# Attention loop of a graph transformer on one core: another order of VectorE's small steps and of the value weighting

## The chip, the cores and the metric

One core of a Trainium2 chip (trn2) runs one program. Its engines are TensorE (PE: matrix products, with a weight load PEld ahead of each), VectorE (DVE), ScalarE (ACT), GpSimd (POOL) and SyncE (SP, which issues DMAs). Each engine takes its own instructions strictly in order and waits for others by semaphores. PE writes to PSUM; a PSUM tile must be read out before its buffer can be written again. The metric is the device time of one execution in microseconds, lower is better.

## What is computed

10,000 nodes, 160,000 edges, 128 features. Seven rounds of normalised propagation over the edges give each node 8 tokens; then one attention block over these 8 tokens, and a readout.

```python
h = x; toks = [x]
for _ in range(7):
    msg = h[src] * deg_inv_sqrt[src, None] * deg_inv_sqrt[dst, None]
    h = segment_sum(msg, dst, N); toks.append(h)
tok = stack(toks, axis=1)                      # (N, 8, D)
t = layernorm(tok)
q, key, v = t @ wq, t @ wk, t @ wv             # per token
attn = softmax(einsum('nkd,nld->nkl', q, key) / sqrt(D))
o = tok + einsum('nkl,nld->nkd', attn, v) @ wo
r = layernorm(o)
alpha = softmax(einsum('nkd,d->nk', r, w_r))
out = einsum('nk,nkd->nd', alpha, o)
```

## The kernel before

The seven propagations (class `Hops`) take the first five sixths of the span and are not touched. The attention stage (function `attention`) works on 625 blocks of 128 rows; a row is one token, so a block is 16 nodes of 8 tokens. Blocks go in groups of `SG` = 16 (the first group has one block): 40 groups, `sgs`.

The order of all engines' work in this stage is the order in which the program states it (`manual_schedule`); tile pools add only the semaphore waits. The loop at the end of `attention` is a software pipeline, `for i in range(-1, n + 5)`. Round `i` handles several groups at once, each at another stage:

- group `i + 3`: `load`, eight DMAs from SP
- group `i + 1`: `xT`, PE transposes `pt`, four blocks in each of four quarters, copied by ACT
- group `i`: `val` (PE `pv`, three blocks at a time, copied by ACT), `uT` (PE `pu`, copied by ACT), `score` (PE `ps`, many small 32x32 products); `squares` on ACT gathers the sums of squares, some of group `i` and some of `i + 1`
- group `i - 1`: the softmax, by small VectorE steps. `soft1a` masks the scores and folds them by two additions, `soft1b` scales by `rk`, takes the maximum and subtracts it, `soft_exp` is ACT's exponential, `soft2` sums, inverts and scales, and has GpSimd spread the result to `p4`; `soft2b` gives the row sums `w`; `soft3` transposes on VectorE and has GpSimd copy four pieces into `PT`
- group `i - 2`: `attend` (PE `po`, value weighting, four blocks in each quarter) and `resid` (VectorE, adds the token; it frees the PSUM buffer of `po`, of which there are two)
- group `i - 3`: `stats`, one `bn_stats` of VectorE for each block; `norms`, `root` (ACT) and `norms2` make the inverse deviations of this group's output and of group `i`'s input
- group `i - 4`: `read1`, `read_exp`, `read2`, the softmax of the readout
- group `i - 5`: `read3` (PE `pf`) and `store`

`same_node` (PE `sm`) sums over the rows of a node: in one PSUM tile first the part that the softmax of group `i - 1` reads (`rb`), then the part that the readout of group `i - 4` reads (`lb`). Its inputs `rb` and `lb` are the last results of `norms2` in the round before.

The four quarters `q` of a round stand on PE in this order, `A0` to `A3` being the four calls of `attend`:

| quarter | PE |
|---|---|
| 0 | pt, pv, sm, pv, pf, pv, A0 |
| 1 | pt, pv, pv, pv, A1 |
| 2 | pt, pu, pu, A2 |
| 3 | pt, pu, pu, A3, ps |

On VectorE the order is: `soft1a`, `soft1b`, eight `bn_stats`, `resid` 0, `soft2`, `soft2b`, `read1`, eight `bn_stats`, `resid` 1, `soft3`, `norms`, `read2`, `norms2`, `resid` 2 and 3.

Of the kernel before, what the change touches and what calls it, by code (L numbers as in the profile page):

```python
# [7 lines left out]
F32 = mybir.dt.float32  # L8
# [5 lines left out]
ALU = mybir.AluOpType  # L14
# [894 lines left out]
def attention(ctx, att, out):  # L909
# [33 lines left out]
    def xT(i, q):  # L943
        a, b = 4 * q, min(4 * q + 4, sgs[i][1])
        if q == 0:
            S[i]["xT"] = tp.tile([128, SG, 128], F32, name="xT")
        if a >= b:
            return
        p = pp.tile([128, 4, 128], F32, name="pt", tag="a", bufs=3)
        for g in range(a, b):  # L950
            T.transpose(p[:, g - a, :], S[i]["x"][:, g, :], ident)  # L951
        A.copy(S[i]["xT"][:, a:b, :], p[:, :b - a])  # L952
# [11 lines left out]
    def val(i, c):  # L964
        a, b = 3 * c, min(3 * c + 3, sgs[i][1])
        if c == 0:
            S[i]["v"] = vp.tile([128, SG, 131], F32, name="v")
        if a >= b:
            return
        p = pp.tile([128, 512], F32, name="pv", tag="a", bufs=3)[:, :393].rearrange("p (g d) -> p g d", d=131)  # L970
        for g in range(a, b):
            T.matmul(p[:, g - a, :], S[i]["xT"][:, g, :], Wv, start=True, stop=True)  # L972
        A.copy(S[i]["v"][:, a:b, :], p[:, :b - a])
# [43 lines left out]
        S[i]["rb"] = r  # L1017


    def soft1a(i):  # L1020
        n = sgs[i][1]
        c = wp.tile([128, SG, 4, 8], F32, name="c4")[:, :n]
        V.tensor_tensor(c, S[i]["s"][:, :n].rearrange("p g (n k) -> p g n k", k=8),
                        in4[:, None, :, None].to_broadcast([128, n, 4, 8]), op=ALU.mult)
        d = wp.tile([128, SG, 2, 8], F32, name="c2")[:, :n]
        V.tensor_tensor(d, c[:, :, 0:2], c[:, :, 2:4], op=ALU.add)
        e = S[i]["e"] = wp.tile([128, SG, 8], F32, name="e")[:, :n]
        V.tensor_tensor(e, d[:, :, 0], d[:, :, 1], op=ALU.add)

    def soft1b(i):  # L1030
        n = sgs[i][1]
        e = S[i]["e"]
        rk = wp.tile([128, SG, 8], F32, name="rk")[:, :n]
        V.tensor_tensor(rk, S[i]["sm"][:, 0, :n], S[i]["rs"][:, :, None].to_broadcast([128, n, 8]), op=ALU.mult)
        V.tensor_mul(e, e, rk)
        m = wp.tile([128, SG], F32, name="m")[:, :n]
        V.tensor_reduce(m, e, axis=X, op=ALU.max)
        V.tensor_tensor(e, e, m[:, :, None].to_broadcast([128, n, 8]), op=ALU.subtract)

    def soft_exp(i):  # L1040
        n = sgs[i][1]
# [4 lines left out]
    def soft2(i):  # L1046
        n = sgs[i][1]
        e = S[i]["e"]
        z = wp.tile([128, SG], F32, name="z")[:, :n]
        V.tensor_reduce(z, e, axis=X, op=ALU.add)  # L1050
        V.reciprocal(z, z)
        V.tensor_tensor(e, e, S[i]["sm"][:, 0, :n], op=ALU.mult)
        V.tensor_tensor(e, e, z[:, :, None].to_broadcast([128, n, 8]), op=ALU.mult)  # L1053
        p = wp.tile([128, SG, 4, 8], F32, name="p4")[:, :n]
        G.tensor_tensor(p, e[:, :, None, :].to_broadcast([128, n, 4, 8]), in4[:, None, :, None].to_broadcast([128, n, 4, 8]), op=ALU.mult)  # L1055
        S[i]["p"] = p

    def soft2b(i):

        n = sgs[i][1]  # L1060
        y = S[i]["y"]
        V.tensor_tensor(y[:, :, :8], S[i]["e"], S[i]["sm"][:, 1, :n], op=ALU.mult)
        w = S[i]["w"] = sp.tile([128, SG], F32, name="w")[:, :n]
        V.tensor_reduce(w, y, axis=X, op=ALU.add)

    def soft3(i):
        n = sgs[i][1]
# [12 lines left out]
    def norms(i, j):  # L1080
        v = sp.tile([128, 2, SG], F32, name="rv")
        if not (ok(i) and ok(j)) or min(sgs[i][1], sgs[j][1]) < SG:
            V.memset(v, 1.0)
        if ok(i):
            n = sgs[i][1]
            d = sp.tile([128, SG], F32, name="rx")[:, :n]
            V.tensor_mul(d, S[i]["v"][:, :n, 130], S[i]["v"][:, :n, 130])
            V.scalar_tensor_tensor(v[:, 0, :n], S[i]["sq"][:, :n], 1.0 / D, d, op0=ALU.mult, op1=ALU.subtract)
        if ok(j):
            n = sgs[j][1]  # L1090
            st = S[j]["st"][:, :n]
            d = sp.tile([128, SG], F32, name="rd")[:, :n]
            V.tensor_tensor(d, st[:, :, 1], st[:, :, 4], op=ALU.subtract)
            V.scalar_tensor_tensor(d, d, 0.25, d, op0=ALU.mult, op1=ALU.mult)
            V.tensor_tensor(v[:, 1, :n], st[:, :, 2], st[:, :, 5], op=ALU.add)
            V.scalar_tensor_tensor(v[:, 1, :n], v[:, 1, :n], 1.0 / D, d, op0=ALU.mult, op1=ALU.add)
        V.tensor_scalar(v, v, 1e-5, None, op0=ALU.add)
        return v

# [20 lines left out]
    def read1(i):  # L1120
        n = sgs[i][1]
        lc = S[i]["lc"]
        m = wp.tile([128, SG], F32, name="rm")[:, :n]
        V.tensor_reduce(m, lc, axis=X, op=ALU.max)
        e = S[i]["re"] = wp.tile([128, SG, 9], F32, name="re")[:, :n]
        V.tensor_tensor(e[:, :, :8], lc, m[:, :, None].to_broadcast([128, n, 8]), op=ALU.subtract)
        V.tensor_tensor(e[:, :, 8], S[i]["l"], m, op=ALU.subtract)

    def read_exp(i):
        A.activation(S[i]["re"], S[i]["re"], AF.Exp)  # L1130
# [36 lines left out]
    load(1)  # L1167
    for i in range(-1, n + 5):

        if ok(i + 3):  # L1170
            load(i + 3)
        if ok(i - 1):
            soft1a(i - 1)
        for q in range(4):
            if ok(i + 1):
                xT(i + 1, q)
            if q == 0 and i < 0:
                A.preload_act_table_set("natural_log_exp_and_others")

            cs = range(3 * q, 3 * q + 3) if q < 2 else ()  # L1180
            if ok(i):
                for c in cs[:1]:
                    val(i, c)
            if q == 0:
                if ok(i):
                    squares(i, 9, 11)
                sm = pp.tile([128, 4, SG * 8], F32, name="sm", tag="m", bufs=1).rearrange("p a (g k) -> p a g k", k=8)
                if ok(i - 1):
                    S[i - 1]["sm"] = sm
                    m = sgs[i - 1][1]  # L1190
                    same_node(sm[:, 0:2, :m], S[i - 1]["rb"][:, :, :m])
                if ok(i - 4):
                    m = sgs[i - 4][1]
                    S[i - 4]["lc"] = sm[:, 2, :m]
                    same_node(sm[:, 2, :m], S[i - 4]["lb"][:, :m])
                if ok(i - 1):
                    soft1b(i - 1)
            if ok(i):
                for c in cs[1:2]:
                    val(i, c)  # L1200
            if q == 0:
                if ok(i):
                    squares(i, 11, 12)
                if ok(i - 1):
                    soft_exp(i - 1)
                if ok(i):
                    squares(i, 12, 13)
                if ok(i - 5):
                    read3(i - 5)
            elif q == 1 and ok(i - 5):  # L1210
                store(i - 5)
            if ok(i):
                for c in cs[2:]:
                    val(i, c)
            if q == 0 and ok(i):
                squares(i, 13, 15)
            if q == 1 and ok(i - 4):
                read_exp(i - 4)
            if q == 1 and ok(i):
                squares(i, 15, 16)  # L1220

            for c in range(2 * q - 4, 2 * q - 2) if q >= 2 else ():
                if ok(i):
                    uT(i, c)
                if c == 3:
                    vy.append(root(vy[0]))
                if ok(i + 1):
                    squares(i + 1, *((0, 2), (2, 3), (3, 4), (4, 9))[c])
            if ok(i - 2):
                attend(i - 2, q)  # L1230
            if q == 3 and ok(i):
                score(i)

            if q < 2 and ok(i - 3):
                stats(i - 3, 8 * q, 8 * q + 8)
            if q == 2:
                vy = [norms(i, i - 3)]
                if ok(i - 4):
                    read2(i - 4)
            if q == 3:  # L1240
                norms2(i, i - 3, *vy)
                if ok(i - 2):
                    resid(i - 2, 2)
            if q != 2 and ok(i - 2):
                resid(i - 2, q)
            if q == 0 and ok(i - 1):
                soft2(i - 1)
                soft2b(i - 1)
            if q == 0 and ok(i - 4):
                read1(i - 4)  # L1250
            if q == 1 and ok(i - 1):
                soft3(i - 1)

@with_exitstack
def nagphormer_kernel(ctx, tc, x, src, dst, dis, wq, wk, wv, wo, w_r, out):
# [42 lines left out]
```

## Time and profile before

| | |
|---|---|
| median of 3 runs | 3991.8 us (3988.98 to 3993.97) |
| profiled execution | 3999.62 us, its span 3997.8 us |
| mean granted TensorE clock in it | 0.973 |
| busy: PE, DVE, ACT, POOL | 94%, 83%, 68%, 44% of the span |

The page cuts the span in 40 equal slices; the attention stage is the last seven. Rows of the timeline read: start in us from the span's beginning, duration of the run of equal instructions in us, engine, line of the kernel, operation, output<-inputs, shapes, count; in brackets the idle time of the engine ahead of it and what ended it. A block of f32 products takes two instructions on PE, so `x8` is four blocks. An end on PE is modelled: the next row may start before it. Tiles that lie in the hop tables' memory are named `tab` (the tokens `x` and the outputs `o`).

### The profile page before, as it was taken

Reading aid. Unit: us, or ns where it says so; the run is one execution under the profiler, and the core shown is the slowest. Engines: PE = TensorE matmul, PEld = TensorE weight load, DVE = VectorE, ACT = ScalarE, POOL = GpSimd, SP = SyncE. Lnnn points to the kernel's source line nnn. Section 1 sums busy time; section 2 is a strip of 40 time slices with the busy share of each in tenths; the row PEclk is TensorE's granted clock in tenths of the full one; section 3 lists DMA queues with packets and bytes.
Section 4 is the critical chain, followed back from the end, with each engine's and each line's share of the span. In section 5 each row is a group of like instructions: output and inputs, shape, how many; then the busy total and the mean of one; then the engine's idle time right before and its main releaser. Section 6 shows DMA issues by size and latency. Waiting matters only on the chain.

```text
span 3997.8 us, 165094 instructions
## 1 busy us (share of the span) xinstructions
PE 3745.5 (94%) x69690; PEld 3031.4 (76%) x69690; DVE 3322.9 (83%) x6961; ACT 2724.5 (68%) x6830; POOL 1766.6 (44%) x2342
## 2 busy tenths in 40 slices
PE   6886799999989999999999999999999999999997
PEld 4665566666658888888888788878878887788885
DVE  8998999999977777777777777777766666999998
ACT  6884456666666666666666666666665658888884
POOL 0000333333335665666666566656656662222222
PEclk8998899999999999999999999999999999999998
DMA  3100445454556666666666666666656552222220
GB/s 104 32 2 1 134 151 154 149 162 143 156 168 189 201 201 193 202 203 200 193 202 202 185 202 202 202 189 198 202 184 205 186 183 77 74 74 76 78 78 13
DMA packets 321189, 594.93 MB, mean 149 GB/s; under 512 B 56183, under 2 KB 214101, under 8 KB 315189
## 3 DMA queue, kind: packets, MB, share of 16 engines
q1 hardware_dynamic: 282485, 506.62, 40.0%
q0 software_dynamic: 35392, 72.55, 6.3%
q8 instruction: 546, 8.95, 0.9%
q10 hardware_dynamic: 2560, 5.12, 0.4%
q14 instruction: 206, 1.69, 0.1%
HBM read 455.43 MB, written 128.67 MB: 146 GB/s over the span
## 4 chain that ended last, share of the span: by engine, by line
PE 71%; DVE 19%; ACT 4%; issue 2%; DMA 2%; POOL 0%; another core or an unknown queue 0%; SPq 0%; DVEq 0%; ACTq 0%; POOLq 0%
PE p L580 26%; PE acc L556 24%; PE acc L542 4%; DVE w L514 3%; PE pv L972 3%; PE po L983 3%; PE pu L961 3%; DVE ux L219 2%; DVE o L212 2%; ACT rs L340 2%; PE tb L440 2%; PE pt L951 1%; DVE oh L206 1%; DVE R L212 1%; DVE w L511 1%
## 5 line engine op out<-in xcount | busy, mean ns | idle before, releaser
L585 ACT CAST eb<-p 128x512 f16<-128x512 f32 x3065 | 1623.7, 596 | 645.4 <-PE p L580 404.3
L587 DVE TENSOR_TENSOR eb<-p,one 128x512 f16<-128x512 f32 x1912 | 1230.6, 685 | 332.2 <-PE acc L556 195.9
L580 PE MATMUL p<-tab,w 128*32 128x256 f16 x39816 | 1288.7, 274 | 44.2 <-issue 21.4
L556 PE MATMUL acc<-eb,w 128*128 128x256 f16 (+1 forms) x9954 | 1246.9, 274 | 8.4 <-DVE indeg L649 3.1
L580 PEld LDWEIGHTS <-w 128*32 128x32 fp8e4 x39816 | 1002.3, 96 | 261.3 <-issue 225.8
L556 PEld LDWEIGHTS <-w 128*128 128x128 fp8e4 x9954 | 954.3, 98 | 170.3 <-issue 54.9
L526 POOL DMA_INDIRECT og<-tabh,oidx x553 | 613.3, 1109 | 767.7 <-DVE vi L478 389.6
L526 POOL DMA_INDIRECT og<-tabd,oidx x541 | 586.3, 1084 | 640.2 <-PE acc L556 294.3
L625 POOL TENSOR_SCALAR r<-s,ctok 128x128 f32<-128x128 f32 x474 | 294.3, 621 | 47.7 <-DVE s L571 30.3
L616 ACT ACTIVATE tab<-s,c 128x128 f16<-128x128 f32 x395 | 158.6, 402 | 209.7 <-DVE eb L587 185.6
L617 DVE SCALAR_TENSOR_TENSOR tab<-s,c,tab 128x128 f16<-128x128 f32 x395 | 138.9, 352 | 180.8 <-issue 168.0
L571 DVE TENSOR_REDUCE s<-acc 128x128 f32<-128x256 f32 x553 | 228.7, 414 | 24.0 <-PE acc L569 11.2
L997 ACT ACTIVATE junk<-tab 128x128 f32<-128x128 f32 x625 | 245.1, 394 | 0.0
L340 ACT ACTIVATE rs<-iof,rb 128x128 fp8e4<-128x128 f32 x784 | 231.8, 389 | 0.3
L514 DVE TENSOR_TENSOR w<-dsl,iof 128x2432 fp8e4<-128x2432 f16 x79 | 211.5, 2678 | 0.0
L983 PEld LDWEIGHTS po<-v,pT 128*128 128x128 f32 x1250 | 159.5, 194 | 42.1 <-issue 27.7
L525 POOL COPY og<-eb 128x1 f16<-128x1 f16 x452 | 83.9, 186 | 241.7 <-ACT eb L585 241.7
L1055 POOL TENSOR_TENSOR p<-e,in 128x512 f32<-128x512 f32 (+1 forms) x40 | 40.8, 1020 | 321.0 <-DVE e L1053 321.0
L972 PE MATMUL pv<-Wv,xT 128*128 128x131 f32 x1250 | 176.7, 285 | 1.3 <-ACT xT L952 0.6
L983 PE MATMUL po<-v,pT 128*128 128x128 f32 x1250 | 167.0, 277 | 5.5 <-DVE tab L989 4.1
L972 PEld LDWEIGHTS pv<-Wv,xT 128*128 128x128 f32 x1250 | 154.2, 192 | 17.9 <-issue 8.8
L542 PE MATMUL acc<-og,w 128*128 128x256 f16 x553 | 156.8, 284 | 0.0
(285 smaller groups left out, 4611.9 us busy)
## 6 DMA issues: line engine op xcount, KB each, us to landing
w<-gsd SPq DMA_DIRECT2D x474, 592.0 KB
gsd<-w SPq DMA_DIRECT2D x79, 592.0 KB
rb<-srow SPq DMA_DIRECT2D x79, 576.0 KB
tok<-r SPq DMA_DIRECT2D x546, 64.0 KB
tab<-tok SPq DMA_DIRECT2D x273, 128.0 KB
tabd<-tab SPq DMA_DIRECT2D x396, 64.0 KB
og<-tabh,oidx POOLq DMA_INDIRECT x553
og<-tabd,oidx POOLq DMA_INDIRECT x541
```

Of the source, the lines that this page charges most:

```text
L340: A.activation(ro[:, j - a, i, :], self.iof, AF.Abs_reciprocal_sqrt, scale=2.0 ** 21, bias=rb[:, j - VP, i:i + 1], saturate=False)
L514: V.tensor_tensor(w[:, :NJ * 128].rearrange("p (j d) -> p j d", d=128), dsl[:, g, :, None].to_broadcast([128, NJ, 128]), self.iof1[:, None ...
L526: self.nc.gpsimd.indirect_dma_start(out=o, out_offset=None, in_=src[0] if i == NI else src[1], in_offset=bass.IndirectOffsetOnAxis(ap=self ...
L542: T.matmul(acc[0][:, :256], W, og[i], start=start, stop=stop)
L556: T.matmul(acc[0][:, :m], w[:, J * 128:(J + 1) * 128], e[:, j, :m], start=first and J == 0, stop=J == NG - 1 and not (first or late))
L580: T.matmul(p[32 * q:32 * q + 32, j], w[:, NJ * 128 + s * CAP:NJ * 128 + (s + 1) * CAP], tab[:, s, :], start=True, stop=True)
L585: A.copy(e[:, :n, 0:256], pv)
L587: V.tensor_tensor(e[:, :n, 0:256], pv, self.one[:, :, None].to_broadcast([128, n, 256]), op=ALU.mult)
L625: self.nc.gpsimd.tensor_scalar(r, s, ct[:, t:t + 1], None, op0=ALU.mult)
L972: T.matmul(p[:, g - a, :], S[i]["xT"][:, g, :], Wv, start=True, stop=True)
L983: T.matmul(p[:, g - a, :], PT[i % 2][:, g, :], S[i]["v"][:, g, :128], start=True, stop=True)
L997: A.activation(j, S[i]["x"][:, g, :], AF.Square, bias=S[i]["x"][:, g, 0:1], scale=-1.0, accum_out=S[i]["sq"][:, g:g + 1])
```

## The change

Nothing is computed otherwise. What changes is where steps stand:

- `soft1a` and `soft1b` become one list of steps `soft1`, stated behind `same_node`. `rk`, which reads `sm`, moves from behind both additions to ahead of them.
- `soft1`, `soft2`, `soft2b` and `read1` return their steps as lists. `fill` states them one by one with one `bn_stats` behind most of them: `bn(m)` states the next `m` of the group's sixteen. Ten stand there; one is stated ahead of `soft3`, and the last five behind it, while GpSimd copies its four pieces.
- In `soft2` the product `e` times `sm` moves ahead of the reciprocal. `read1` moves ahead of `soft2`. In `norms` the steps of the two groups alternate.
- `attend` opens each quarter instead of ending it; `score` comes directly behind the last `uT`.
- `resid` 0 comes behind `soft2b`, `resid` 1 behind the last `bn_stats`, `resid` 2 ahead of `norms`, `resid` 3 ahead of `norms2`.

| quarter | PE after |
|---|---|
| 0 | A0, pt, pv, sm, pv, pf, pv |
| 1 | A1, pt, pv, pv, pv |
| 2 | A2, pt, pu, pu |
| 3 | A3, pt, pu, pu, ps |

The core of the diff, with the new loop in place of the old one (the old one is printed above):

```diff
-    def soft1a(i):
...
-    def soft1b(i):
...
+    def soft1(i):
...
+        return (
+            lambda: V.tensor_tensor(c, S[i]["s"][:, :n].rearrange("p g (n k) -> p g n k", k=8),
+                                    in4[:, None, :, None].to_broadcast([128, n, 4, 8]), op=ALU.mult),
+            lambda: V.tensor_tensor(rk, S[i]["sm"][:, 0, :n], S[i]["rs"][:, :, None].to_broadcast([128, n, 8]), op=ALU.mult),
+            lambda: V.tensor_tensor(d, c[:, :, 0:2], c[:, :, 2:4], op=ALU.add),
+            lambda: V.tensor_tensor(e, d[:, :, 0], d[:, :, 1], op=ALU.add),
+            lambda: V.tensor_mul(e, e, rk),
+            lambda: V.tensor_reduce(m, e, axis=X, op=ALU.max),
+            lambda: V.tensor_tensor(e, e, m[:, :, None].to_broadcast([128, n, 8]), op=ALU.subtract))
...
+        return (lambda: V.tensor_reduce(z, e, axis=X, op=ALU.add),
+                lambda: V.tensor_tensor(e, e, S[i]["sm"][:, 0, :n], op=ALU.mult),
+                lambda: V.reciprocal(z, z),
+                last)
...
+        def bn(m):
+            a, b = done[0], min(16, done[0] + m)
+            done[0] = b
+            if ok(i - 3) and a < b:
+                stats(i - 3, a, b)
+
+        def fill(steps, ms):
+
+            for step, m in zip(steps, ms):
+                step()
+                bn(m)
...
+        if ok(i - 2):
+            attend(i - 2, 0)
+        if ok(i + 1):
+            xT(i + 1, 0)
...
+        if soft:
+            fill(soft1(i - 1), (0, 0, 1, 1, 1, 1, 0))
...
+        bn(2)
+        if read:
+            fill(read1(i - 4), (1, 0, 0))
+        if soft:
+            fill(soft2(i - 1), (0, 1, 1, 0))
+            fill(soft2b(i - 1), (1, 0))
+        if ok(i - 2):
+            resid(i - 2, 0)
+
+        if ok(i - 2):
+            attend(i - 2, 1)
...
+        bn(1)
+        if soft:
+            soft3(i - 1)
+        bn(16)
+        if ok(i - 2):
+            resid(i - 2, 1)
...
+        if ok(i - 2):
+            attend(i - 2, 2)
+        if ok(i + 1):
+            xT(i + 1, 2)
+        if ok(i - 2):
+            resid(i - 2, 2)
+        vy = [norms(i, i - 3)]
+        if read:
+            read2(i - 4)
+        u((0, 1))
+
+        if ok(i - 2):
+            attend(i - 2, 3)
+        if ok(i + 1):
+            xT(i + 1, 3)
+        u((2, 3))
+        if ok(i):
+            score(i)
+        if ok(i - 2):
+            resid(i - 2, 3)
+        norms2(i, i - 3, *vy)
```

More of the change, by code (lines that the diff above doesn't have):

```diff
@@ L1049, in soft2, with last @@
         z = wp.tile([128, SG], F32, name="z")[:, :n]
[L1050 to L1056, printed above, removed]
+        p = S[i]["p"] = wp.tile([128, SG, 4, 8], F32, name="p4")[:, :n]
+        def last():
+            V.tensor_tensor(e, e, z[:, :, None].to_broadcast([128, n, 8]), op=ALU.mult)
+            G.tensor_tensor(p, e[:, :, None, :].to_broadcast([128, n, 4, 8]), in4[:, None, :, None].to_broadcast([128, n, 4, 8]), op=ALU.mult)
+        return (lambda: V.tensor_reduce(z, e, axis=X, op=ALU.add),
+                lambda: V.tensor_tensor(e, e, S[i]["sm"][:, 0, :n], op=ALU.mult),
+                lambda: V.reciprocal(z, z),
+                last)
     def soft2b(i):
@@ L1061, in soft2b @@
         y = S[i]["y"]
-        V.tensor_tensor(y[:, :, :8], S[i]["e"], S[i]["sm"][:, 1, :n], op=ALU.mult)
         w = S[i]["w"] = sp.tile([128, SG], F32, name="w")[:, :n]
-        V.tensor_reduce(w, y, axis=X, op=ALU.add)
+        return (lambda: V.tensor_tensor(y[:, :, :8], S[i]["e"], S[i]["sm"][:, 1, :n], op=ALU.mult),
+                lambda: V.tensor_reduce(w, y, axis=X, op=ALU.add))
     def soft3(i):
@@ L1083, in norms @@
             V.memset(v, 1.0)
+        if ok(j):
+            m = sgs[j][1]
+            st = S[j]["st"][:, :m]
+            f = sp.tile([128, SG], F32, name="rd")[:, :m]
+            V.tensor_tensor(f, st[:, :, 1], st[:, :, 4], op=ALU.subtract)
         if ok(i):
@@ L1087, in norms @@
             V.tensor_mul(d, S[i]["v"][:, :n, 130], S[i]["v"][:, :n, 130])
+        if ok(j):
+            V.scalar_tensor_tensor(f, f, 0.25, f, op0=ALU.mult, op1=ALU.mult)
+            V.tensor_tensor(v[:, 1, :m], st[:, :, 2], st[:, :, 5], op=ALU.add)
+        if ok(i):
             V.scalar_tensor_tensor(v[:, 0, :n], S[i]["sq"][:, :n], 1.0 / D, d, op0=ALU.mult, op1=ALU.subtract)
         if ok(j):
[L1090 to L1096, printed above, removed]
+            V.scalar_tensor_tensor(v[:, 1, :m], v[:, 1, :m], 1.0 / D, f, op0=ALU.mult, op1=ALU.add)
         V.tensor_scalar(v, v, 1e-5, None, op0=ALU.add)
@@ L1123, in read1 @@
         m = wp.tile([128, SG], F32, name="rm")[:, :n]
-        V.tensor_reduce(m, lc, axis=X, op=ALU.max)
         e = S[i]["re"] = wp.tile([128, SG, 9], F32, name="re")[:, :n]
-        V.tensor_tensor(e[:, :, :8], lc, m[:, :, None].to_broadcast([128, n, 8]), op=ALU.subtract)
-        V.tensor_tensor(e[:, :, 8], S[i]["l"], m, op=ALU.subtract)
+        return (lambda: V.tensor_reduce(m, lc, axis=X, op=ALU.max),
+                lambda: V.tensor_tensor(e[:, :, :8], lc, m[:, :, None].to_broadcast([128, n, 8]), op=ALU.subtract),
+                lambda: V.tensor_tensor(e[:, :, 8], S[i]["l"], m, op=ALU.subtract))
     def read_exp(i):
@@ L1168, in attention @@
     for i in range(-1, n + 5):
+        done = [0]
+        def bn(m):
[7 more added lines that the diff above has]
+                bn(m)
+        soft, read = ok(i - 1), ok(i - 4)
         if ok(i + 3):
             load(i + 3)
[L1172 to L1222, printed above, removed]
@@ new lines, in attention @@
+        if ok(i - 2):
+            attend(i - 2, 0)
+        if ok(i + 1):
+            xT(i + 1, 0)
+        if i < 0:
+            A.preload_act_table_set("natural_log_exp_and_others")
+        if ok(i):
+            val(i, 0)
+            squares(i, 9, 11)
+        sm = pp.tile([128, 4, SG * 8], F32, name="sm", tag="m", bufs=1).rearrange("p a (g k) -> p a g k", k=8)
+        if soft:
+            S[i - 1]["sm"] = sm
+            m = sgs[i - 1][1]
+            same_node(sm[:, 0:2, :m], S[i - 1]["rb"][:, :, :m])
@@ new lines, in attention @@
+        if read:
+            m = sgs[i - 4][1]
+            S[i - 4]["lc"] = sm[:, 2, :m]
+            same_node(sm[:, 2, :m], S[i - 4]["lb"][:, :m])
+        if soft:
+            fill(soft1(i - 1), (0, 0, 1, 1, 1, 1, 0))
+        if ok(i):
+            val(i, 1)
+            squares(i, 11, 12)
+        if soft:
+            soft_exp(i - 1)
+        if ok(i):
+            squares(i, 12, 13)
+        if ok(i - 5):
+            read3(i - 5)
+        if ok(i):
+            val(i, 2)
+            squares(i, 13, 15)
@@ new lines, in attention @@
+        bn(2)
+        if read:
+            fill(read1(i - 4), (1, 0, 0))
+        if soft:
+            fill(soft2(i - 1), (0, 1, 1, 0))
[5 more added lines that the diff above has]
+        if ok(i + 1):
+            xT(i + 1, 1)
+        if ok(i):
+            val(i, 3)
+            val(i, 4)
+        if ok(i - 5):
+            store(i - 5)
+        if ok(i):
+            val(i, 5)
+        if read:
+            read_exp(i - 4)
@@ L1223, in attention, with u @@
+        if ok(i):
+            squares(i, 15, 16)
+        bn(1)
+        if soft:
+            soft3(i - 1)
+        bn(16)
+        if ok(i - 2):
+            resid(i - 2, 1)
+        def u(cs):
+            for c in cs:
                 if ok(i):
@@ L1228, in attention @@
                     squares(i + 1, *((0, 2), (2, 3), (3, 4), (4, 9))[c])
[L1229 to L1252, printed above, removed]
+        if ok(i - 2):
[5 more added lines that the diff above has]
+        vy = [norms(i, i - 3)]
+        if read:
+            read2(i - 4)
+        u((0, 1))
+        if ok(i - 2):
+            attend(i - 2, 3)
+        if ok(i + 1):
+            xT(i + 1, 3)
+        u((2, 3))
+        if ok(i):
+            score(i)
+        if ok(i - 2):
+            resid(i - 2, 3)
+        norms2(i, i - 3, *vy)
 @with_exitstack
```

10 lines of the change are left out of this document (removed).

## The prediction

> **What bounds the kernel now.** The edit lies in the attention stage alone: the loop over 40 groups that ends the span. Each turn of it is called a round here. I read its waits on PE first, over the steady rounds.
>
> ```profile
> PE pt L951 <- PE ps L1003: 7.2, 34, 0.3
> PE sm L1009 <- issue: 0.4, 1, 0.4
> ```
>
> The columns are total us, times, longest. In 563 us of steady rounds PE waits for no other engine at all: only for a pause behind its own score products `ps`, once a round. So PE sets the pace, and the pace is read where `sm` starts, once a round, in the first steady round and 35 rounds on.
>
> ```profile
> 3372.55 0.64 PE L1009 MATMUL sm<-rb,same 128*32 128x256 f32 x8
> ...
> 3937.08 0.42 PE L1009 MATMUL sm<-rb,same 128*32 128x256 f32 x4
> ```
>
> That is 564.53 us for 35 rounds, 16.13 us each. What PE does in one of them is in its timeline (start, duration, operation). `po` is value weighting, A0 to A3 below.
>
> ```profile
> 3603.65 1.05 PE L983 MATMUL po<-v,pT 128*128 128x128 f32 x8
> ...
> 3609.75 1.05 PE L983 MATMUL po<-v,pT 128*128 128x128 f32 x8
> 3610.73 1.30 PE L1003 MATMUL ps<-xT,uT 128*32 128x32 f32 x128
> 3612.24 0.63 PE L951 MATMUL pt<-ident,tab 128*128 128x128 f32 x4 [0.22 <-PE ps L1003]
> 3612.71 0.83 PE L972 MATMUL pv<-Wv,xT 128*128 128x131 f32 x6
> 3613.47 0.64 PE L1009 MATMUL sm<-rb,same 128*32 128x256 f32 x8
> 3613.93 0.40 PE L1009 MATMUL sm<-lb,same 128*32 128x128 f32 x8
> 3614.26 0.94 PE L972 MATMUL pv<-Wv,xT 128*128 128x131 f32 x6
> 3615.13 1.08 PE L1151 MATMUL pf<-tab,Ab 128*32 128x128 f32 x32
> 3616.14 0.94 PE L972 MATMUL pv<-Wv,xT 128*128 128x131 f32 x6
> 3616.91 1.05 PE L983 MATMUL po<-v,pT 128*128 128x128 f32 x8
> 3617.80 0.60 PE L951 MATMUL pt<-ident,tab 128*128 128x128 f32 x4
> 3618.24 1.73 PE L972 MATMUL pv<-Wv,xT 128*128 128x131 f32 x14
> 3619.81 1.05 PE L983 MATMUL po<-v,pT 128*128 128x128 f32 x8
> ```
>
> Every row starts where the one before it ends: there is no slack on PE. DVE is nearly as full, and its small steps are what the edit reorders; the same round on DVE:
>
> ```profile
> 3614.74 0.42 DVE L1026 TENSOR_TENSOR c<-c 128x256 f32<-128x256 f32 x1
> 3615.20 0.29 DVE L1028 TENSOR_TENSOR e<-c 128x128 f32<-128x128 f32 x1
> 3615.41 0.28 DVE L1034 TENSOR_TENSOR rk<-sm,ry 128x128 f32<-128x128 f32 x1
> 3615.73 0.29 DVE L1035 TENSOR_TENSOR e<-e,rk 128x128 f32<-128x128 f32 x1
> ...
> 3616.59 1.64 DVE L1078 BATCH_NORM_STATS2 st<-tab 128x6 f32<-128x128 f32 x8
> 3618.14 0.67 DVE L989 TENSOR_TENSOR tab<-po,tab 128x512 f32<-128x512 f32 x1
> 3618.73 0.27 DVE L1050 TENSOR_REDUCE z<-e 128x16 f32<-128x128 f32 x1
> 3619.04 0.25 DVE L1051 RECIPROCAL z<-z 128x16 f32<-128x16 f32 x1
> 3619.21 0.23 DVE L1052 TENSOR_TENSOR e<-e,sm 128x128 f32<-128x128 f32 x1
> 3619.47 0.29 DVE L1053 TENSOR_TENSOR e<-e,z 128x128 f32<-128x128 f32 x1
> 3619.80 0.29 DVE L1062 TENSOR_TENSOR y<-e,sm 128x128 f32<-128x128 f32 x1
> 3620.12 0.30 DVE L1064 TENSOR_REDUCE w<-y 128x16 f32<-128x144 f32 x1
> 3620.34 0.28 DVE L1124 TENSOR_REDUCE rm<-sm 128x16 f32<-128x128 f32 x1
> ```
>
> Two spacings are to be seen. `e` L1028 and `rk` L1034 do not depend on each other and start 0.21 us apart, though the first takes 0.29. `rk` and L1035, which reads it, are 0.32 apart. A statistics step (`bn_stats`) costs 1.55/8 = 0.194 us (3616.59 to 3618.14). So a dependent pair holds DVE for 0.11 us that an independent step put between them would use.
>
> **The change, part by part.**
>
> (1) Statistics between dependent steps. Ten of the sixteen `bn_stats` now stand in `soft1`, `read1`, `soft2` and `soft2b`, and about nine gaps of 0.11 us go: 1.0 us of DVE in a round. On PE's path that is worth nothing while PE waits for no DVE step, as the first fence shows. But it makes the softmax chain longer from end to end, since ten times 0.194 now lie inside it, and part (3) puts that chain where PE waits for it.
>
> [...]
>
> (2) Order on PE. The cyclic order of PE stays the same but for one exchange: before, it was last `pu`, A3, `ps`, `pt`; after, it is last `pu`, `ps`, A0 of the next round, `pt`. The pause behind `ps` belongs to four queue instructions that wait for the DMAs of `x` ahead of `pt`:
>
> ```profile
> L951 PEldq EVENT_SEMAPHORE  x4: 51/51/51, 3611.8 to 3612.1; - x4
> ```
>
> In the last round with products, whose `pv` follows `ps` directly, there are none of these:
>
> ```profile
> 3934.82 1.30 PE L1003 MATMUL ps<-xT,uT 128*32 128x32 f32 x128
> 3936.05 0.94 PE L972 MATMUL pv<-Wv,xT 128*128 128x131 f32 x6
> ```
>
> `ps` to the next start is 1.23 there and 1.51 with them: 0.28 us. After the change they stand behind A0, whose 0.89 us (3616.91 to 3617.80) can hide them. A0 has one such instruction of its own (0.05), and pays for leaving the narrow `ps` shape: six `pv` behind `pf` take 3616.91 - 3616.14 = 0.77, where the fourteen from 3618.24 to 3619.81 run at 0.112 each, so 0.10. I take -0.28 + 0.05 + 0.10 = -0.13 us a round; the ends are -0.28 (all goes) and +0.05 (the four still show, and A0's own comes on top).
>
> (3) Value weighting one place earlier, `resid` later. A2 needs the PSUM buffer of A0 (two buffers), so it waits for `resid` 0. Before, `resid` 0 ends at 3618.14 + 0.67 = 3618.81 and A2 is two places behind 3619.81's A1: over 3 us of slack. After, A2 has the place that A1 has now, 3619.81, while `resid` 0 moves on DVE from ahead of `z` to behind `w`. I walk that, counting from `sm`'s start.
>
> - `rk` is now the second step of `soft1`, ahead of both additions, and waits for the whole of `sm`, whose one signal follows the `lb` half: 3613.93 + 0.40 - 3613.47 = 0.86, and 0.06 to wake DVE (below). So 0.92.
> - From `rk` to `resid` 0: ten `bn_stats`, 1.94. Fifteen steps: `rk` 0.21, the 128x256 addition 0.34 (0.42 less the 0.08 by which the next may start early), `e`, product and maximum 0.21 each, subtraction 0.21, `read1` 0.20, 0.21 and 0.09 (the last has a sixteenth of the elements; an estimate), `z` 0.31 (the next step overwrites what it reads, so it waits), `e` times `sm` 0.15, reciprocal 0.17, `last` 0.33, `y` 0.21, `w` 0.22: 3.28. Together 5.22.
> - `resid` 0 itself 0.67, waking PE 0.06.
>
> That gives 0.92 + 5.22 + 0.73 = 6.87 us after `sm` starts. PE by itself reaches A2's place 3619.81 - 3613.47 = 6.34 after it. So PE waits 0.53 us in each round, in a place where it waited for nothing. The wake-up of 0.06 is from the tail, where nothing else is queued:
>
> ```profile
> 3986.74 0.65 PE L1009 MATMUL sm<-lb,same 128*32 128x128 f32 x8 [6.65 <-DVE lb L1114]
> 3987.45 0.29 DVE L1124 TENSOR_REDUCE rm<-sm 128x16 f32<-128x128 f32 x1 [0.86 <-PE sm L1009]
> ```
>
> Queued behind the waiting A2 on PE are two `pt`, four `pu`, A3 and the score, and so everybody. The loop closes through them: A2 to the end of the last `pu` is 3609.75 - 3603.65 = 6.10 (the same six blocks, in the same order), from there to `sm` the four blocks of 3609.75 to 3613.47, 3.72 less 0.13. The new round is 6.87 + 6.10 + 3.59 = 16.56 us. PE alone would need 6.34 + 6.10 + 3.59 = 16.03.
>
> The ends: the walk on DVE may be 0.25 shorter or longer (one step in twenty-five costed 0.01 wrong gives that), and A2, which cannot load its weights ahead while it waits, may pay 0.10 more. With the ends of (2): 16.2 to 17.1.
>
> (4) Everything else, at nothing, with its cover. `resid` 1 ends some 2.5 us behind `resid` 0 (six `bn_stats` 1.16, a transpose of the same size and itself, 0.67 each), and A3 stands 3.05 us behind A2 (half of the six blocks of 6.10 us, which repeat after three). `soft_exp` on ACT has all of `read1` to finish in. GpSimd's copies of `pT` start behind that transpose, some 9 us after `sm`, and A0 asks for them 15 us after it. The regrouped `norms` ends before ACT's last `uT` copy, which the root stands behind in both orders. Were one of these late, PE would wait by so much more a round.
>
> (5) The tail, 3937.08 to 3986.74, has no `pt`, then no products, and DVE sets it. There the gaps do pay: up to 1.0 us in each of four rounds, less what `rk` waits for `sm`. I take -2, the ends are 0 and -4.
>
> **Sum.** 35 rounds at 16.56 are 579.6; less 0.46 for the `pt` that round 39 lacks and about 0.4 for a first round with a readout of one group: 578.7, against 564.53. That is +14.2, with the tail +12.2. The profiled execution took 3999.62 us for its span of 3997.8, and would take 4011.8. The median of the runs shown is 3991.8, 7.8 below it; the same addition gives 4004.0 us.
>
> A measurement of this kernel tells about 0.2%, 8 us, from no change: faster is below 3983.8, slower above 3999.8.
>
> **Rivals.**
>
> *PE keeps the pace.* If the walk from `sm` to `resid` 0 is at most 6.34 us and not 6.87, A2 never waits, and the round is PE's own 16.03: 35 rounds give 561.1 - 0.9 - 564.5 = -4.3, with the tail -6.3: 3985.5, from 3981 to 3990. For it: DVE has no idle time to lose and 1.0 us less to do. Against it: the wait for all of `sm`, which can't begin before PE is there. The point of decision is 0.53 us of slack. Chance 0.20; half of it is faster by over 8 us.
>
> *The cover of part (2) is missing.* The four queue instructions show behind A0 as they do behind `ps`, and A2 loads its weights late: 16.56 + 0.18 + 0.10 = 16.84, 35 rounds give +24.0, with the tail +22: 4013.8. For it: behind `ps` nothing hides them. Against it: eight products of 0.11 stand ahead of them now. Chance 0.14.
>
> *The gaps are not gaps.* If each step flushed in full, the fifteen steps would take their durations and 0.03 (4.7 in all) and the ten `bn_stats` 0.31 each (0.28 for the last of eight: 1.64 - 7 x 0.194): 7.8 in place of 5.22, a round of 19.1 and over 4080 us. [...] Chance 0.03. Then the edit would not do what it says.
>
> **How the numbers follow.** The forecast, a round between 16.3 and 16.75, has 0.63; it gives 3995 to 4011, and about a fifth of it lies within 8 us of no change. Faster: half of the first rival and a little, 0.11. Same: the other half and that fifth, 0.23. Slower: the rest, 0.66. The range 3985 to 4016 leaves out half of the first rival, the third, and the upper part of the second: some 0.18.
>
> **What would show it.** Right: `sm` starts 16.4 to 16.7 us apart; the waits name `po` on PE or PEld behind DVE's L989 some 35 times at about 0.5 us; `rk` idles behind `sm` on DVE; the pause of `pt` behind `ps` is gone. Wrong: rounds of 16.0 with no such wait (first rival), or `pt` still idle behind `po` (second), or `bn_stats` 0.3 us apart from their neighbours (third). If rounds are as forecast and the total is not, the tail is mis-sized.

## The result: slower by half a per cent, and the profile after

| | before | after |
|---|---|---|
| median of 5 runs each | 3992.61 us (3988.98 to 4000.94) | 4013.27 us (4009.73 to 4015.8) |
| profiled execution, its span | 3999.62, 3997.8 us | 4015.77, 4014.0 us |
| busy: PE, DVE | 94%, 83% | 94%, 81% |

The ratio after to before is 1.0049, 95% interval 1.0035 to 1.0064. Slower was forecast, with 4004.0 us and a range of 3985 to 4016; the time came out near the upper end of the range. One term of the sum was too small, and by more than the ends that the prediction gave it.

PE's waits in the steady rounds of the kernel after (total us, times, longest), and what VectorE waits for at `rk`:

```profile
DVE rk L1031 <- PE sm L1009: 43.0, 33, 1.4
PEld po L983 <- DVE tab L989: 19.4, 34, 0.9
PE po L983 <- DVE tab L989: 12.8, 34, 0.7
```

Before, PE waited for no other engine. Now it waits 34 times for `resid` (L989), and VectorE idles 1.3 us a round until `sm` comes. The same two places in the timeline as before give the pace, `sm` of the first steady round and of the one 35 rounds on:

```profile
3369.75 0.64 PE L1009 MATMUL sm<-rb,same 128*32 128x256 f32 x8
...
3957.93 0.64 PE L1009 MATMUL sm<-rb,same 128*32 128x256 f32 x8
```

588.18 us instead of 564.53: +23.65, where +14.2 was forecast. Most rounds take 16.88 to 16.93, a few 16.7. From there to the last `sm`, 4002.68, it is 44.75 us instead of 49.66: -4.9, where -2 was forecast. The stretch ahead of the first steady round is 2.8 shorter in this execution, what follows the last `sm` 0.26 longer: +16.2 in all, as the spans say. The medians differ by 20.7, which is 4.5 more: the profiled execution of the kernel before lay 7.0 us above its median, that of the kernel after 2.5.

One round on PE, from `sm` to the next `sm`:

```profile
3604.98 0.64 PE L1009 MATMUL sm<-rb,same 128*32 128x256 f32 x8
...
3611.84 1.16 PE L983 MATMUL po<-v,pT 128*128 128x128 f32 x8 [0.36 <-DVE tab L989]
3612.84 0.60 PE L951 MATMUL pt<-ident,tab 128*128 128x128 f32 x4
3613.27 1.88 PE L961 MATMUL pu<-xT,M 128*128 128x512 f32 x4
3614.99 1.05 PE L983 MATMUL po<-v,pT 128*128 128x128 f32 x8
3615.88 0.60 PE L951 MATMUL pt<-ident,tab 128*128 128x128 f32 x4
3616.32 1.88 PE L961 MATMUL pu<-xT,M 128*128 128x512 f32 x4
3618.13 1.62 PE L1003 MATMUL ps<-xT,uT 128*32 128x32 f32 x128
3619.68 1.16 PE L983 MATMUL po<-v,pT 128*128 128x128 f32 x8
3620.68 0.60 PE L951 MATMUL pt<-ident,tab 128*128 128x128 f32 x4
3621.12 0.84 PE L972 MATMUL pv<-Wv,xT 128*128 128x131 f32 x6
3621.88 0.64 PE L1009 MATMUL sm<-rb,same 128*32 128x256 f32 x8
```

Three things are to be seen. A2 (3611.84) waits for `resid` 0 and starts 6.86 us behind `sm`. It then holds PE for 1.00 (to 3612.84), where A3, which waited for nothing, holds it for 0.89. And the score block holds PE for 1.55 (3618.13 to 3619.68), where it took 1.23 before. In the last four rounds that have this block it takes 1.22 to 1.23 again:

```profile
3921.79 1.30 PE L1003 MATMUL ps<-xT,uT 128*32 128x32 f32 x128
3923.01 1.16 PE L983 MATMUL po<-v,pT 128*128 128x128 f32 x8
```

By then no `x` load is left to issue. Those rounds last 16.58 us and less.

VectorE in the same round, a few of its rows:

```profile
3605.91 0.29 DVE L1031 TENSOR_TENSOR rk<-sm,ry 128x128 f32<-128x128 f32 x1 [1.36 <-PE sm L1009]
...
3606.65 0.28 DVE L1033 TENSOR_TENSOR e<-c 128x128 f32<-128x128 f32 x1
3606.84 0.28 DVE L1079 BATCH_NORM_STATS2 st<-tab 128x6 f32<-128x128 f32 x1
3607.04 0.28 DVE L1034 TENSOR_TENSOR e<-e,rk 128x128 f32<-128x128 f32 x1
...
3611.10 0.69 DVE L989 TENSOR_TENSOR tab<-po,tab 128x512 f32<-128x512 f32 x1
```

The product with `rk` (L1034) starts 0.39 us behind the step it depends on, and a `bn_stats` ran in between: two operations in 0.39 us, where a dependent pair alone took 0.32 before. The gaps are filled as meant.

### The profile page after: what moved, and what is told of

Its sections match the earlier page's. It is cut to its first block, busy times and chain, and to the rows that moved or that the text cites. A ratio compares the mean times of both kernels' runs of the same rounds, so it can differ in the third digit from the quotient of the medians.

```text
span 4014.0 us, 165131 instructions
## 1 busy us (share of the span) xinstructions
PE 3753.2 (94%) x69690; PEld 3029.3 (75%) x69690; DVE 3251.4 (81%) x6961; ACT 2725.7 (68%) x6830; POOL 1773.2 (44%) x2342
## 4 chain that ended last, share of the span: by engine, by line
PE 68%; DVE 23%; ACT 3%; DMA 2%; issue 2%; DVEq 0%; another core or an unknown queue 0%; SPq 0%; ACTq 0%; POOL 0%; POOLq 0%
PE p L580 25%; PE acc L556 24%; PE acc L542 4%; DVE w L514 3%; PE pu L961 3%; PE po L983 3%; DVE ux L219 2%; DVE o L212 2%; DVE st L1079 2%; ACT rs L340 2%; DVE oh L206 1%; PE tb L440 1%; DVE R L212 1%; PE ps L1003 1%; PE pt L951 1%
## 5 line engine op out<-in xcount | busy, mean ns | idle before, releaser
L983 PE MATMUL po<-v,pT 128*128 128x128 f32 x1250 | 175.0, 284 | 20.7 <-DVE tab L989 20.6
```

What stands on the lines that cost most here:

```text
L983: T.matmul(p[:, g - a, :], PT[i % 2][:, g, :], S[i]["v"][:, g, :128], start=True, stop=True)
```

## The experiments

All ratios are to the kernel before, run beside the variant on the same chip, with 95% intervals. Four of them (each part alone, `resid` 0 early, the loads behind the store) shared one chip, on which the kernel before takes 3992.39 us, four others a chip on which it takes 3941.66, and the last two had a chip each (3940.91 and 3998.95). So ratios are compared, and the lengths of rounds.

### PE's order and VectorE's lists, each alone

First the interleaving alone, with `attend` at the end of each quarter and `resid` 2 and 3 behind `norms2`, as before:

```diff
-        if ok(i - 2):
-            attend(i - 2, 1)
         if ok(i + 1):
             xT(i + 1, 1)
...
             squares(i, 15, 16)
+        if ok(i - 2):
+            attend(i - 2, 1)
         bn(1)
```

> VectorE's part of the change alone: statistics stated between the dependent steps as in the kernel after, soft3 ahead of resid 1, the norm steps reordered; but value weighting back at the end of each quarter, score behind the last of them, resid 2 and 3 back behind the second half of the norms. Theory B (before is bound by PE, and the ten gaps of 0.11 that the statistics fill are VectorE's alone): rounds stay at 16.1, only the last rounds get shorter, 3989 us (3985 to 3993). Rival G (the gaps lie on the path): 1.0 us a round, 3957. Rival I (the interleaving, by its longer chain from sm, is what made the kernel slower): 4010.

Measured: 3990.22 us, ratio 0.9995 (0.9987 to 1.0004). Rounds are 16.10 to 16.17, as before. PE's one steady wait is the old pause behind `ps`:

```profile
PE pt L951 <- PE ps L1003: 6.8, 33, 0.3
```

So the filled gaps are worth nothing while PE sets the pace (theory B), and the interleaving does no harm by itself. From the `sm` that answers to 3937.08 (3938.89 here) to the last it takes 46.79 us instead of 49.66: -2.9 in the tail.

Then PE's order alone, with VectorE's lists untouched:

```diff
         for q in range(4):
+            if ok(i - 2):
+                attend(i - 2, q)
             if ok(i + 1):
                 xT(i + 1, q)
...
-            if ok(i - 2):
-                attend(i - 2, q)
             if q == 3 and ok(i):
                 score(i)
```

> PE's part of the change alone: value weighting first in each quarter and score directly behind the last pu block, with VectorE's list as before (resid 0 behind eight statistics, resid 2 and 3 behind the second half of the norms). Theory R (the additions set what the earlier weighting costs; with two buffers of po A0 must now wait for resid 2, which ends 14.2 us behind rk, 0.9 + 14.2 + 0.1 + 2.3 us from sm to sm): rounds 17.5, 35 rounds by 1.4, about 4040 us (4020 to 4055). Rival O (the order on PE by itself is harmless, and only the interleaving's longer chain costs): rounds 16.0 to 16.2, 3985 to 3993.

Measured: 4093.41 us, ratio 1.0258 (1.0243 to 1.0272), rounds of 18.5 to 19.7. Theory R has the place right (A0 waits for `resid` 2) and the size too small. A0's row on PE, then `rk` and `resid` 2 (with 3 behind it) on VectorE:

```profile
3608.50 1.42 PE L983 MATMUL po<-v,pT 128*128 128x128 f32 x8 [2.16 <-DVE tab L989]
```

```profile
3593.45 0.29 DVE L1034 TENSOR_TENSOR rk<-sm,ry 128x128 f32<-128x128 f32 x1 [1.26 <-PE sm L1009]
...
3607.67 1.28 DVE L989 TENSOR_TENSOR tab<-po,tab 128x512 f32<-128x512 f32 x2
```

`resid` 2 ends at 3608.31, 14.9 us behind `rk` and not 14.2, since the norms now wait 0.9 for ACT's root: 18.2 for a round. The rest is the clock. Windows of the same round; PEclk is the third number from the end, the first PE number is its busy time:

```profile
3606.40:3608.50 2.10, 0.00 (x0) 0.03 (x1) 2.00 (x8) 1.66 (x10) 0.00 (x0) 1.00 0.04 8
3608.50:3609.20 0.70, 0.70 (x6) 0.70 (x7) 0.70 (x2) 0.00 (x0) 0.00 (x0) 1.00 0.00 0
3609.20:3612.40 3.20, 3.20 (x18) 2.78 (x21) 1.07 (x3) 0.86 (x2) 0.00 (x0) 0.50 0.55 154
3612.40:3612.80 0.40, 0.40 (x12) 0.24 (x8) 0.00 (x0) 0.40 (x2) 0.00 (x0) 0.74 0.28 82
```

After 2.16 us of idle PE, and 0.7 us into A0, the granted clock falls to 0.50 for some 3.4 us, and A0, `pt`, `pv` and `sm` stretch. It does not follow every such pause: of three rounds read in a row, two show it and one does not, which fits the uneven round lengths. The Trainium skill (TensorE: Matmul & The Clock Gate, "Part 1: The HAM clock gate") puts the gate's window at about 3.4 us and lets it run freely, not from the start of a pause; the 3.4 us at half clock and the pauses that it misses agree with that. Its table of states asks for an idle window of that length, though, and here 2.16 us of idle were enough.

So the change's two parts lean on each other: PE's order alone costs 2.6%, and what repairs most of it is not the interleaving but where the additions stand. That was tried by itself, VectorE's lists not interleaved, `resid` 0 first in the round, `resid` 2 ahead of the norms and 3 behind them:

```diff
+        if ok(i - 2):
+            attend(i - 2, 0)
+        if ok(i - 2):
+            resid(i - 2, 0)
         if ok(i - 1):
             soft1a(i - 1)
...
+            if q == 2 and ok(i - 2):
+                resid(i - 2, 2)
             if q == 2:
                 vy = [norms(i, i - 3)]
```

> PE's part of the change with VectorE's steps not interleaved (lists as before: eight statistics at a time, dependent steps behind each other), but the additions where PE's new order needs them: resid 0 first in the round, resid 2 ahead of the norms, resid 3 behind them. Theory V (without the interleaving VectorE's list of a round is 16.1 to 16.2 us with no idle time in it, as in the kernel before, so PE's 15.9 to 16.1 can't show): rounds 16.15 to 16.3, 3990 to 3995 us. Rival (the interleaving gives nothing here either): rounds 15.94 to 16.08, 3980 to 3985.

Measured: 0.9984 (0.9975 to 0.9993), rounds 16.03 to 16.04. That is the rival, nearly. VectorE's list, "full" before, shrank with the order: of the four norm steps that took 0.51 to 0.64 us beside GpSimd's copies, the last (L1097) now starts behind the copies in most rounds and takes 0.18 instead of 0.64. What is left of theory V is 0.09 us a round against the best version below. A3 misses `resid` 1 by a hair (`resid` 1 ends at 3564.35):

```profile
3563.68 0.67 DVE L989 TENSOR_TENSOR tab<-po,tab 128x512 f32<-128x512 f32 x1
```

```profile
3564.43 1.14 PE L983 MATMUL po<-v,pT 128*128 128x128 f32 x8
```

It holds PE for 0.98 instead of 0.89: its first weight load starts at 3564.41, with the product and not ahead of it.

### The wait of A2 for `resid` 0

Theory W was that this wait, made by the longer list from `sm` to `resid` 0, is the main cost. Three edits shorten that list in different ways. First, `resid` 0 moved into VectorE's idle time ahead of `rk`:

```diff
+        if ok(i - 2):
+            resid(i - 2, 0)
         if soft:
             fill(soft1(i - 1), (0, 0, 1, 1, 1, 1, 0))
...
             fill(soft2b(i - 1), (1, 0))
-        if ok(i - 2):
-            resid(i - 2, 0)
```

> The kernel after, with the addition resid 0 moved on VectorE from behind the softmax steps to ahead of c4 and rk, where VectorE idles 1.4 us a round until sm; nothing else. Theory W (A2 waits for resid 0, 0.53 us a round and another 0.10 because its first weights can't be loaded ahead): A2 starts 6.3 us behind sm instead of 6.86 and takes 0.89, rounds 16.25, 34 rounds by 0.63, so about 3992 us (score block unchanged at 1.55). Rival N (another wait takes its place: resid 1 before A3, pT before A0, or rb before sm): the round stays above 16.6 and the time above 4003.

Measured: 3984.55 us, 0.9980 (0.9972 to 0.9989); on another chip again:

> The kernel with resid 0 early once more, on the same chip as the run without loads, for the comparison: rounds 16.08, ps to po 1.36 in most rounds, 0.998 of before.

0.9981 (0.9971 to 0.999). Rounds are 16.08, and A2 starts 6.33 us behind `sm`, PE's own pace:

```profile
3612.41 0.64 PE L1009 MATMUL sm<-rb,same 128*32 128x256 f32 x8
...
3618.74 1.05 PE L983 MATMUL po<-v,pT 128*128 128x128 f32 x8
```

One move of one addition makes the change 0.2% faster than before. Of the 0.82 us that the round loses, 0.63 was expected. The other 0.19 is the score block, which took 1.36 instead of 1.55 without being touched.

Second, a dose: `resid` 0 ahead by one step only.

```diff
             fill(soft2(i - 1), (0, 1, 1, 0))
-            fill(soft2b(i - 1), (1, 0))
+            weigh, total = soft2b(i - 1)
+            weigh()
+            bn(1)
         if ok(i - 2):
             resid(i - 2, 0)
+        if soft:
+            total()
```

> The kernel after, with resid 0 moved ahead by one step only, in front of the sum w (0.29 us). A dose of the same cure: theory W: A2 starts 6.57 us behind sm instead of 6.86, its wait falls from 0.52 to 0.23 and its eight products still take 1.00; the loads are issued 0.56 ahead of the score block, so by theory H one lands in it, 1.36 instead of 1.55: rounds 16.44, 34 rounds by 0.45, 3998 us; without H 16.6, 4003 us. If the wait is all or nothing: 4013 or 3985.

Measured: 1.0015 (1.0006 to 1.0024), which is 3998 us where the kernel before takes 3992.4; rounds 16.41, A2 6.56 us behind `sm`:

```profile
3545.46 0.64 PE L1009 MATMUL sm<-rb,same 128*32 128x256 f32 x8
...
3552.02 1.16 PE L983 MATMUL po<-v,pT 128*128 128x128 f32 x8
```

One step of 0.29 us less in the list takes 0.30 us off A2's start: the wait shrinks by what the list loses, and the 1.00 for A2's products stays. Third, `rk` moved back behind the two additions and their two statistics:

```diff
-            lambda: V.tensor_tensor(rk, S[i]["sm"][:, 0, :n], ...),
             lambda: V.tensor_tensor(d, c[:, :, 0:2], c[:, :, 2:4], op=ALU.add),
             lambda: V.tensor_tensor(e, d[:, :, 0], d[:, :, 1], op=ALU.add),
+            lambda: V.tensor_tensor(rk, S[i]["sm"][:, 0, :n], ...),
...
-            fill(soft1(i - 1), (0, 0, 1, 1, 1, 1, 0))
+            fill(soft1(i - 1), (0, 1, 1, 0, 1, 1, 0))
```

> The kernel after, with the product rk (the first step that needs sm) moved on VectorE from ahead of the two additions to behind them, as in the kernel before, with their two statistics; resid 0 stays where it is. Theory W (A2 waits for resid 0 because the list from sm to resid 0 is too long): the additions and two statistics run before sm, 0.8 us leaves the list, resid 0 starts 5.3 us behind sm instead of 6.1, the wait of 0.5 is gone. The score block: in the kernel after the loads' first issue is 0.85 us ahead of it and it takes 1.55 us to po, in the run with resid 0 early 0.58 ahead and 1.36, with no load 1.22. Theory H (each 128 KB load that lands in the block costs about 0.15): here the issue comes about 1.0 ahead of it, two loads land in it, 1.55; rounds 16.27, 3992 us. Rival H2 (the block's length has nothing to do with when the loads land): 1.36 as in the run with resid 0 early, rounds 16.08, 3985.

Measured: 0.9991 (0.9982 to 1.0), rounds 16.18; PE's wait for `resid` is gone. So it is the length of the list that counts, not where `resid` 0 stands in it: W holds. The score block took 1.46 to 1.48 in most rounds, between H's 1.55 and H2's 1.36; the price of 0.15 for each landing load is not exact.

### The score block and the loads

In the kernel after, `resid` 3 ends ahead of the score block and releases the `x` buffer, so SP issues the next set's eight loads 0.85 us ahead of the block; in the kernel before the first issue came 3.3 us behind the block's start. What SP's queue waits for at the loads, then `resid` 3 and the first load of the round shown:

```profile
SPq L854 <- DVE tab L989: 116.3, 30, 5.3
```

```profile
3616.57 0.68 DVE L989 TENSOR_TENSOR tab<-po,tab 128x512 f32<-128x512 f32 x1
```

```profile
3617.28 0.56 SPq L854 DMA_DIRECT2D tab<-in_x  x1
```

Windows of 0.2 us through it (the second pair in a row is PEld, weight loads; at the end DMA share and GB/s):

```profile
3618.40:3618.60 0.20, 0.20 (x47) 0.20 (x35) 0.00 (x0) 0.20 (x1) 0.00 (x0) 1.00 0.00 0
3618.60:3618.80 0.20, 0.20 (x39) 0.20 (x28) 0.00 (x0) 0.20 (x2) 0.00 (x0) 1.00 2.41 614
3618.80:3619.00 0.20, 0.20 (x32) 0.18 (x21) 0.00 (x0) 0.17 (x3) 0.00 (x0) 1.00 0.15 41
3619.00:3619.20 0.20, 0.20 (x39) 0.20 (x36) 0.00 (x0) 0.20 (x2) 0.00 (x0) 1.00 0.31 82
3619.20:3619.40 0.20, 0.20 (x37) 0.20 (x24) 0.14 (x1) 0.20 (x2) 0.00 (x0) 1.00 1.24 328
```

Weight loads run at 35 in 0.2 us, fall to 28 and then to 21 as the first load lands (614 GB/s), come back to 36, and fall again with the second. The granted clock is 1.00 throughout.

The 32 steady rounds of the same kernel show a dose. Where the DMA queues moved 0.13 MB during the block, which is one load, it took 1.35 to 1.38 us (five blocks). Where they moved 0.23 to 0.26 MB, about two loads, it took 1.52 to 1.57, in all of 23 blocks but one (1.36). The four blocks in between took either length.

The first attempt to part the loads from the block moved them behind the store:

```diff
-        if ok(i + 3):
-            load(i + 3)
...
             store(i - 5)
+        if ok(i + 3):
+            load(i + 3)
```

> The kernel after, with the eight x loads of set i+3 stated on SP behind the store of the round instead of at its top, so that they no longer land during the score block. Theory L (the loads landing during the 128 small score products hold PE back: 1.55 us from ps to po with them, 1.22 in the last three rounds, which have no load): ps to po 1.23, rounds 16.58 instead of 16.9, some 33 rounds by 0.3, so about 4003 us. Rival P (score directly behind the last pu block costs 0.3 by itself, or waits for ScalarE's copies of uT): ps to po stays 1.55, 4013.

Measured: 4009.97 us, 1.0047 (1.0034 to 1.006), rounds 16.73, `ps` to `po` 1.37 to 1.40 in most. The edit missed its aim, so it decides nothing: eight issues take SP some 5 us, and the last ones still fall into the block, which starts at 3613.01:

```profile
3606.86 1.42 SPq L1165 DMA_DIRECT2D out<-f  x2
3608.37 0.56 SPq L854 DMA_DIRECT2D tab<-in_x  x1
3608.98 4.37 SPq L854 DMA_DIRECT2D tab<-tok  x7
```

The second attempt kept `resid` 0 early and put `resid` 3 behind the second half of the norms, so that the loads are released behind the block:

```diff
-        if ok(i - 2):
-            resid(i - 2, 3)
         norms2(i, i - 3, *vy)
+        if ok(i - 2):
+            resid(i - 2, 3)
```

> The kernel with resid 0 early, and resid 3 moved behind the second half of the norms, where the kernel before has it: its end releases the x buffer, so the loads are issued behind the score block, not during it. Theory H (loads that land in the score block hold it up, 0.15 us each): ps to po 1.22 in all rounds instead of 1.36, rounds 15.94, 31 rounds by 0.14, 3980 us. Rival P (score behind the last pu block costs 0.14 by itself and the loads nothing): 1.36, 3984.5. Rival D (VectorE's list from the norms to rk gets too long: resid 3 0.6, resid 0 0.6 and c4 0.7 behind rb, 1.1 of it idle before): rk late, rounds above 16.2, over 3988.

Measured: 0.9972 (0.9963 to 0.9981), rounds 15.94, the block 1.22 to 1.23 in nearly all of them, the loads' first issue 3.3 us behind its start:

```profile
3569.10 1.30 PE L1003 MATMUL ps<-xT,uT 128*32 128x32 f32 x128
3570.32 1.16 PE L983 MATMUL po<-v,pT 128*128 128x128 f32 x8
```

```profile
3572.43 0.57 SPq L854 DMA_DIRECT2D tab<-in_x  x1
```

This is the fastest version that computes the same: 3929.69 us where before takes 3941.66. It moves `resid` 3 and the loads at once, so one more run, again with `resid` 0 early, left `resid` 3 where the kernel after has it and took the loads away from set 7 on. Those sets compute on what the six `x` buffers already hold instead of their own tokens; every other instruction stays. (A version without the loads from set 6 on gave no time.) The part that concerns the loads:

```diff
         if ok(i + 3):
-            load(i + 3)
+            if i + 3 < 7:
+                load(i + 3)
+            else:
+                S[i + 3]["x"] = att.x(i + 3)
```

> The kernel with resid 0 early (resid 3 ahead of the score block as in the kernel after), without the x loads from set 7 on: those sets compute on what the six x buffers already hold, so their values are not the reference's; every other instruction stays. It tells whether the block's 1.36 us in that kernel comes from the loads or from where resid 3 stands. Theory H (the loads): ps to po 1.22 in all rounds behind the first few, rounds 15.94, 30 rounds by 0.14, 4.2 us less than the kernel with resid 0 early, about 0.9970 of before. Rival R3 (resid 3 ahead of the block, whatever it releases): 1.36 in most rounds, rounds 16.08, 0.998 of before.

Measured: 0.9965 (0.9955 to 0.9975), rounds 15.94, the block 1.22 to 1.23 in nearly all. It is the loads. Together (offset is the first issue against the block's start; values of most rounds):

| kernel | offset | `ps` to `po` | round |
|---|---|---|---|
| after | -0.85 us | 1.52 to 1.57 us | 16.9 us |
| `rk` back | -1.01 | 1.46 to 1.48 | 16.18 |
| `resid` 0 by one step | -0.64 | 1.35 to 1.37 | 16.41 |
| `resid` 0 early | -0.58 | 1.35 to 1.37 | 16.08 |
| loads behind the store | -4.64 | 1.37 to 1.40 | 16.73 |
| `resid` 0 early, 3 late | +3.33 | 1.22 to 1.23 | 15.94 |
| no loads | none | 1.22 to 1.23 | 15.94 |

What stays open is how a landing load holds up PE's small products: a few rounds have traffic in the block and still take 1.23, so the traffic alone does not do it every time, and no run here shows what it meets. The loading of instructions is not it in general: in 19 of the 24 steady blocks of the kernel after that take 1.52 us or more, the queues that load instructions moved nothing.

## Why the prediction was right, and which term was too small

- **(1) The gaps.** Filled, and worth nothing on PE's path: 0.9995 alone. The third rival, by which each step flushes in full, would have made the rounds 19.1 us; the spacings of 0.19 to 0.20 us between independent steps speak against it again. The Trainium skill (VectorE: DVE Perf Modes, "The DRAIN you can't avoid") states such a flush behind every operation, but adds that a next operation which is not held starts earlier; these spacings, with steps of 0.28 us, agree with what it adds.
- **(2) The pause behind `ps`.** Gone as forecast. Its four queue instructions now stand behind A0, while A0's products run (3619.68 to 3620.68):

```profile
L951 PEldq EVENT_SEMAPHORE  x4: 51/51/51, 3619.6 to 3620.0; - x4
```

  Undisturbed, PE's order is worth a little more than the forecast -0.13: 15.94 against 16.13, -0.19.
- **(3) A2 and `resid` 0.** The steps of the walk, forecast and measured: `sm` to `rk` 0.92 and 0.93, `rk` to `resid` 0 5.22 and 5.19, A2 behind `sm` 6.87 and 6.86. (Two slips beside it cost nothing: before, A2 stands one place behind A1, not two, and the last step of `read1` has an eighth of the elements, not a sixteenth.) Its late weights, in the forecast only as an end (0.10), are there in every round: 1.00 instead of 0.89.
- **The term that was mis-sized** is the stretch from the last `pu` to `sm`, 3.59 us forecast and 3.84 measured. For the exchange on PE part (2) took -0.13 with ends of -0.28 and +0.05; it came out at +0.12, beyond them. It was costed by `ps` at its old 1.23 us; it took 1.55. The other blocks there came out 0.07 cheaper. The cause is a step that part (4) put "at nothing" without naming it: `resid` 3 moves ahead of `norms2`, and with it the eight loads that its end releases, into the score block. The order on SP was unchanged, and the release was not followed.
- **The sum of a round**: 16.56 + 0.10 + 0.32 - 0.07 = 16.91; measured 16.88 to 16.93.
- **(5) The tail**: -4.9, beyond the end of -4. The gaps give -2.9 (interleaving alone). PE's order with early additions, without the interleaving, takes 46.92 us from 3875.47 to its last `sm`, -2.7. That part was not in the sum. The two misses have opposite signs: the 35 rounds came out 9.5 us longer than forecast, the tail 2.9 shorter. Without the tail's 2.9 the time would have been 4016, the upper end of the range; that it lies inside is in part luck.
- **Rivals.** "PE keeps the pace" failed at its point of decision: the list is 0.5 us longer than PE's own 6.34; it becomes true once the list is cut by more than that. "The cover is missing" named 4013.8, close to the result, but by a mechanism that did not occur: nothing showed behind A0. The smaller part of its surcharge, A2's late weights, did.

## What to carry to other kernels

A step that frees a buffer carries with it everything that the buffer's release sets off: follow it past the engine, to the queue that issues the next load and to what that load then collides with. Filling the gaps of an engine that does not set the pace gained nothing here, and every filler between a result and its reader lengthens the list that another engine may be waiting behind; put the step that frees a buffer first, in the idle time, and the fillers behind it. Here the same idea with two additions moved goes from 0.5% slower to 0.3% faster.

## What the runs showed of the hardware that was not expected

- A block of 128 small products (128*32, 1.22 us) takes 1.35 to 1.38 us when one 128 KB load lands in it and 1.52 to 1.57 when two do, with few exceptions; mechanism open.
- After 2.16 us of idle PE the granted clock fell to 0.50 for about 3.4 us in about two of three rounds, not in all.
- Eight products that had to wait for a semaphore hold PE for 1.00 us instead of 0.89, although the wait is counted apart.
